# Reading counts and lists out of PSUM at once, gathered rows in a ring of tiles, and gathers issued earlier, in a recurrence-and-router kernel

## The chip, the cores and the metric

The kernel runs on one core of a Trainium2 chip. The metric is the device time of one execution in microseconds (us). The core has a matrix engine (TensorE, PE in the profile, with its weight loads on a row of their own, PEld), a vector engine (VectorE, DVE), a scalar engine (ScalarE, ACT), a general engine (GpSimd, POOL) and a queue engine that issues transfers (SyncE, SP). The engines run side by side, each through its own list of instructions in order, and wait for one another where data or buffers demand it. Matrix products land in PSUM, a small memory that DVE and ACT read out; all else lies in SBUF.

## The reference, cut to what matters

Inputs are float32. There are two stages. The first is a linear recurrence over 768 steps for 4 batches and 8 heads of width 48; the second is a router that sends each of the 3072 rows of width 384 to the one of 8 experts with the largest logit, and runs that expert's two layers.

```python
for t in range(S):                                   # S = 768
    kt, vt, rt = (k[:, :, t], v[:, :, t], r[:, :, t])
    cur = np.einsum('bhd,bhe->bhde', u[None] * kt, vt)
    y[:, :, t] = np.einsum('bhd,bhde->bhe', rt, state + cur)
    state = w[None, :, :, None] * state + np.einsum('bhd,bhe->bhde', kt, vt)
x = y.transpose(0, 2, 1, 3).reshape(B * S, H * D)    # 3072 x 384

logits = xn @ en.T / tau                             # xn, en: rows of x and of the embeddings, normalised
expert_idx = np.argmax(logits, axis=1)
gate_w = softmax(logits)[np.arange(N), expert_idx]
for e in range(E):                                   # E = 8
    mask = expert_idx == e
    h = np.maximum(x[mask] @ w1[e], 0.0)             # 384 -> 1024
    out[mask] = gate_w[mask, None] * (h @ w2[e])     # 1024 -> 384
```

## The kernel before

The recurrence is done in 24 units: unit i is chunk i // 4 (128 steps) of batch i % 4. A loop over i works on several units at once at different stages (a software pipeline). After every fourth unit the chunk's 512 rows are routed: `choose` finds the expert, `ranks` the place in that expert's list, `slices` and `taken` put row numbers and gates into the lists (`k.sums`). The rows themselves go to a buffer `xs` in the chip's main memory (`put`), from where each expert gathers its own.

After chunk 3 (unit 15 and those before it), the counts are read once (`counted`, at j = 7) and the two experts with the fewest rows so far (ranks 7 and 6, `LAST`) are settled as the first to run (`settle`). Their weights are loaded during the last units, and the first 128 rows of each ("early" rows) are gathered from `xs` and run through the expert at the loop's end. Then the final lists are made, and the experts run one after the other: the two of `LAST` with their remaining rows, then the six others.

Each tile of PSUM in the first stage comes from `Banks`: a tag has one buffer (two for "tp" and "at"). A new tile with a tag waits until the last reader of the tile before it, with the same tag, is done. The tag "st" is used by `states`, `ranks`, `taken`, `counted` and the first `turned_lists`.

```python
def counted(k):
    cp = k.ps.tile([128, E], F32, name="cp", tag="st")
    k.nc.tensor.matmul(cp, k.ones, k.cum, start=True, stop=True)
    return cp

def order(k, cp, settled=None):
    load = p.tile([128, E], F32, name="load", tag="load")
    nc.vector.tensor_sub(load, cp, k.tie)                     # L582: reads cp
    ...                                                       # key, more, by (L586 to L593)
    return load, by

def settle(k, cp):
    load, by = order(k, cp)
    ...                                                       # settled (L603), expert_of: eq, is_e, who
    nc.vector.tensor_sub(lack, cp[0:1, :], k.ebase)           # L607: reads cp
    ...

def ranks(k, g):
    g.rank = k.ps.tile([128, B, E], F32, name="rank", tag="st")
    mm(g.rank, k.umask, g.oh, start=True, stop=False)         # L496
    ...

def taken(k, g):
    g.take = k.ps.tile([QS, 128], F32, name="take", tag="st")
    ...                                                       # 4 matmuls, L563

def taken_by_rank(k, lists):
    take = tiles(k, lists, E * TM)                            # L833, L835: read lists
    gates = k.const.tile([128, E * TM], F32, name="gates", tag="gates", bufs=2)
    k.nc.vector.tensor_copy(gates, lists[:, 1, :])            # L651: reads lists
    return take, gates

def attention(k):
    for i in range(-1, units + 7):
        ...                                                   # summed, places, own_rows, turn, ...
        whole(choose, i - 3)
        whole(listed, i - 5)
        on(sums, i)
        on(carry, i)
        on(rows, i)
        of_group(put, i)
        on(scores, i + 1)
        on(own_sum, i + 1)
        of_group(turn_rows, i - 1)
        of_group(logits, i - 2)
        whole(ranks, i - 3)
        whole(gates, i - 3)
        whole(taken, i - 5)
        ...
        j = i - SETTLED * B                                   # SETTLED * B = 12
        if j == 7:
            k.cp = counted(k)
        if j == 8:
            settle(k, k.cp)
            for w, r in zip(k.weights, LAST):
                load_weights_of(k, r, w)
        if j == 9:
            perm = turner(k, k.by)
            k.lists = turned_lists(k, perm, "st")             # L644
        if j == 10:
            lists = taken_by_rank(k, k.lists)
            first = [Early(k, r, *lists, w) for r, w in zip(LAST, k.weights)]
            to = outs(k, lists[0], E * TM)
        if i == units - 1:
            for f in first:
                f.turn()
        ...                                                   # first[0]: hidden, rows, out; first[1].hidden(0)
    cp = counted(k)
    loads, by = order(k, cp, k.settled)
    lists = turned_lists(k, turner(k, by), "lg")
    first[1].hidden(1)
    k.take, k.gates = taken_by_rank(k, lists)
    k.to = outs(k, k.take, E * TM)
    first[1].rows(0)
    first[1].rows(1)                                          # L815
    first[1].out(to)                                          # L822 and L823: earlyy to the output
    caps_passed(k, loads, by)
```

`Early` zeroes a tile of its own (L782) and gathers into it (L783). After the first stage its pools are closed, and the pools of the expert stage (`gp`, `xtp`, `hp`) take the same part of SBUF. A gather zeroes its tile on DVE, because rows past the end of a list are not written:

```python
def gather(k, take, to, gate, n=128):
    G = k.gp.tile([128, DM], F32, name="G", tag="G")          # 8 buffers
    nc.vector.memset(G, 0.0)                                  # L856
    nc.gpsimd.indirect_dma_start(out=G[0:n, :], in_=k.xs[:, :], ...)   # L857
    return G, to, gate, n

def expert(k, rows, w1, w2):
    ...
    for m in range(NK):
        for t, (G, _, _, here) in enumerate(rows):
            nc.tensor.transpose(ps[...], G[0:here, ...], k.ident[...])  # L873
        nc.vector.tensor_copy(xT[:, m, 0:n], ps[:, 0:n])               # L876
    ...                                                       # first layer L881, L882; second L899 or L889 to L896
```

Of the kernel before, what the change touches and what calls it, by code (L numbers as in the profile page):

```python
# [19 lines left out]
C = 128  # L20
NCH = S // C
DP = 64
NP = H // 2
# [22 lines left out]
def build_first(k):  # L46


    nc, pool = k.nc, k.aconst
    wc = pool.tile([128, NP], F32, name="wc")  # L50
    nc.vector.memset(wc, 1.0)
    with nc.allow_non_contiguous_dma(reason="384 words"):
        for s, q in ((0, nc.sync), (1, nc.scalar)):
            q.dma_start(out=wc[s * DP : s * DP + D, :], in_=k.w.rearrange("(p s) d -> s d p", s=2)[s])
    k.ones = k.const.tile([128, 128], F32, name="ones")
    nc.vector.memset(k.ones, 1.0)
    wide = pool.tile([128, 512], F32, name="wide")
    nc.vector.memset(wide, 1.0)
    k.ident = k.const.tile([128, 128], F32, name="ident")
    make_identity(nc, k.ident)  # L60

    def wake(count):
        ps = k.ps.tile([128, 512], F32, name="wake", tag="y")
        for _ in range(count):
            nc.tensor.matmul(ps, k.ones, wide, start=True, stop=True)

    wake(WAKE[0])
    for lst, name, count in ((k.Kpad, "Kpad", 4), (k.Rpad, "Rpad", AHEAD + 2)):
        for i in range(count):
            t = pool.tile([128, H, DP], F32, name=f"{name}{i}")  # L70
            nc.gpsimd.memset(t[:, :, D:DP], 0.0)
            lst.append(t)
    load(k, 0, nc.scalar)


    nc.vector.tensor_scalar(wc, wc, W_MIN, W_MAX, ALU.max, ALU.min)
    t = pool.tile([128, NP, C], F32, name="wpow")
    for p in range(NP):
        nc.vector.tensor_tensor_scan(
            t[:, p, :], wc[:, p : p + 1].to_broadcast([128, C]), k.ones, 1.0, ALU.mult, ALU.mult  # L80
        )
    mid = pool.tile([128, NP], F32, name="mid")
    nc.vector.reciprocal(mid, t[:, :, C // 2])
    over_i = mid[:, :, None].to_broadcast([128, NP, C])
    kp = pool.tile([128, NP, C], F32, name="kp")
    nc.vector.tensor_mul(kp, t[:, :, ::-1], over_i)
    ps = k.ps.tile([128, NP, 2, DP], F32, name="kpT", tag="xp")
    for p in range(NP):
        nc.tensor.transpose(ps[:, p].rearrange("q s d -> q (s d)"), kp[:, p, :], k.ident)
    wake(WAKE[1])  # L90
    k.rpow = pool.tile([128, NP, C], F32, name="rpow")
    nc.vector.tensor_mul(k.rpow, t, over_i)
    cols = ps[:, :, :, 0:D]
    nc.vector.tensor_mul(
        k.Kpad[0].rearrange("q (p s) d -> q p s d", s=2)[:, :, :, 0:D],
        k.loaded[0][0].rearrange("q (p s) d -> q p s d", s=2), cols,
    )
    k.kpow = pool.tile([128, H, D], F32, name="kpow")
    nc.vector.tensor_copy(k.kpow.rearrange("q (p s) d -> q p s d", s=2), cols)  # L99
    k.wC = t[:, :, C - 1 : C].to_broadcast([128, NP, D])  # L100
# [10 lines left out]
def build_consts(k):  # L111
# [35 lines left out]
    k.turned = numbers(k, "turned", [QS, QS], [[0, 2], [1, E], [0, TM]], 1, 0)  # L147
    k.part = pool.tile([QS, 1], I32, name="part")
    nc.gpsimd.iota(k.part, pattern=[[0, 1]], base=0, channel_multiplier=1)
    k.caps = pool.tile([1, E], F32, name="caps")  # L150
    for i, cap in enumerate(CAPS):
        nc.gpsimd.memset(k.caps[:, i : i + 1], float(cap))
# [50 lines left out]
def build_experts(k):  # L203

    nc, pool = k.nc, k.aconst
    emb, tau = k.emb_rows, k.tau_rows
    sq = pool.tile([E, DM], F32, name="emb_sq")
    nrm = pool.tile([E, 1], F32, name="emb_nrm")
    nc.scalar.activation(sq, emb, ACT.Square, accum_out=nrm)
    nc.gpsimd.tensor_tensor(out=nrm, in0=nrm, in1=k.half[0:E, 0:1], op=ALU.pow)  # L210
    yield
    nc.vector.tensor_scalar_add(nrm, nrm, 1e-6)
    nc.vector.reciprocal(nrm, nrm)
    nc.vector.reciprocal(tau, tau)
    nc.vector.tensor_scalar(emb, emb, nrm, tau, ALU.mult, ALU.mult)
    yield
    ps = k.ps.tile([128, NK, E], F32, name="ps", tag="xp")
    for c in range(NK):
        nc.tensor.transpose(ps[:, c, :], emb[:, c * 128 : (c + 1) * 128], k.ident[0:E, 0:E])
    k.ent = k.const.tile([128, NK, E], F32, name="ent")  # L220
    nc.vector.tensor_copy(k.ent, ps)
    yield
# [352 lines left out]
    return cp  # L575


def order(k, cp, settled=None):

    nc, p = k.nc, k.rt  # L580
    load = p.tile([128, E], F32, name="load", tag="load")
    nc.vector.tensor_sub(load, cp, k.tie)  # L582
    key = load
    if settled is not None:
        key = p.tile([128, E], F32, name="key", tag="key")
        nc.vector.scalar_tensor_tensor(key, settled, -float(4 * N), load, ALU.mult, ALU.add)  # L586
    more = p.tile([128, E, E], F32, name="more", tag="more")
    full = [128, E, E]
    nc.vector.tensor_tensor(
        more, key[:, None, :].to_broadcast(full), key[:, :, None].to_broadcast(full), ALU.is_gt  # L590
    )
    by = p.tile([128, E], F32, name="by", tag="by")
    nc.vector.reduce_sum(by, more, axis=AX.X)  # L593
    return load, by


def settle(k, cp):


    nc, pool = k.nc, k.const  # L600
    load, by = order(k, cp)
    k.settled = pool.tile([128, E], F32, name="settled")
    nc.vector.tensor_scalar(k.settled, by, float(min(LAST)) - 1, None, ALU.max)  # L603
    expert_of(k, by)
    k.by = by
    lack = pool.tile([1, E], F32, name="lack")
    nc.vector.tensor_sub(lack, cp[0:1, :], k.ebase)  # L607
    nc.vector.tensor_scalar(lack, lack, -1.0, 128.0, ALU.mult, ALU.add)
    last = pool.tile([1, E], F32, name="last")
    nc.vector.tensor_scalar(last, by[0:1], float(min(LAST)), None, ALU.is_ge)  # L610
    nc.vector.scalar_tensor_tensor(lack, lack, 0.0, last, ALU.max, ALU.mult)
    nc.vector.tensor_add(k.cum[0:1], k.cum[0:1], lack)
# [74 lines left out]
def attention(k):  # L687
# [4 lines left out]
    def on(f, i):  # L692
        if 0 <= i < units:
            f(k, i)
# [8 lines left out]

    emb = build_experts(k)
    for i in range(-1, units + 7):
        if 0 < i + AHEAD < units:
            load(k, i + AHEAD)
        if i < 2:
# [8 lines left out]
        of_group(squares, i - 1)  # L717
        whole(choose, i - 3)
        whole(listed, i - 5)
        on(sums, i)  # L720
        on(carry, i)
        on(rows, i)
# [9 lines left out]
            decays(k)  # L732
        if i == 2:
            build_turned(k)
        j = i - SETTLED * B
        if j == 7:
            k.cp = counted(k)
        if j == 8:
            settle(k, k.cp)
            for w, r in zip(k.weights, LAST):  # L740
                load_weights_of(k, r, w)
        if j == 9:
            perm = turner(k, k.by)
            k.lists = turned_lists(k, perm, "st")
        if j == 10:
            lists = taken_by_rank(k, k.lists)
            first = [Early(k, r, *lists, w) for r, w in zip(LAST, k.weights)]
            to = outs(k, lists[0], E * TM)
        if i == units - 1:
            for f in first:  # L750
# [7 lines left out]
        if i == units + 4:  # L758
            first[0].rows(1)
            first[0].out(to)  # L760
            first[1].hidden(0)
    cp = counted(k)
    loads, by = order(k, cp, k.settled)
    lists = turned_lists(k, turner(k, by), "lg")
    first[1].hidden(1)
    k.take, k.gates = taken_by_rank(k, lists)
    k.to = outs(k, k.take, E * TM)
    first[1].rows(0)
    first[1].rows(1)
    first[1].out(to)  # L770
    caps_passed(k, loads, by)


class Early:


    def __init__(self, k, r, take, gates, weights):
        self.k, self.r, self.weights = k, r, weights
        self.col = slice(r * TM, r * TM + 1)
        self.gate = gates[:, self.col]  # L780
        self.G = k.aconst.tile([128, DM], F32, name=f"early{r}")
        k.nc.vector.memset(self.G, 0.0)  # L782
        k.nc.gpsimd.indirect_dma_start(  # L783
            out=self.G[:, :], out_offset=None, in_=k.xs[0 : (SETTLED + 1) * B * C, :],
            in_offset=IndirectOffsetOnAxis(ap=take[:, self.col], axis=0),
# [4 lines left out]
    def turn(self):  # L790
        k, nc = self.k, self.k.nc
        ps = k.ps.tile([128, NK, 128], F32, name="early_x", tag="tp")
        for m in range(NK):
            nc.tensor.transpose(ps[:, m, :], self.G[:, m * 128 : (m + 1) * 128], k.ident)
        self.xT = k.aconst.tile([128, NK, 128], F32, name=f"earlyx{self.r}")
        nc.vector.tensor_copy(self.xT, ps)

    def hidden(self, half):
# [19 lines left out]

    def out(self, to):
        k, nc, ps = self.k, self.k.nc, self.ps  # L820
        y = k.aconst.tile([128, DM], F32, name=f"earlyy{self.r}")
        nc.vector.tensor_scalar_mul(y, ps, self.gate)  # L822
        nc.gpsimd.indirect_dma_start(  # L823
            out=k.out[:, :], out_offset=IndirectOffsetOnAxis(ap=to[:, self.col], axis=0), in_=y[:, :], in_offset=None,
# [27 lines left out]
def gather(k, take, to, gate, n=128):  # L852

    nc = k.nc
    G = k.gp.tile([128, DM], F32, name="G", tag="G")
    nc.vector.memset(G, 0.0)  # L856
    nc.gpsimd.indirect_dma_start(  # L857
        out=G[0:n, :], out_offset=None, in_=k.xs[:, :], in_offset=IndirectOffsetOnAxis(ap=take[0:n], axis=0),
        bounds_check=N - 1, oob_is_err=False,
    )  # L860
    return G, to, gate, n


def expert(k, rows, w1, w2):
# [146 lines left out]
def kernel(  # L1011
# [47 lines left out]
    with ExitStack() as ctx2:  # L1059
        expert_pools(n, ctx2)  # L1060
        for i, r in enumerate(TURN):
            at = [
                gather(n, *(a[:, j : j + 1] for a in (n.take, n.to, n.gates)), min(128, CAPS[r] - t))
                for t, j in zip(range(0, CAPS[r], 128), range(r * TM, (r + 1) * TM))
                if t > 0 or r not in LAST
            ]
            expert(n, at, *n.weights.pop(0))
            if i + 2 < E:
                n.weights.append(weight_tiles(n))
                load_weights_of(n, TURN[i + 2], n.weights[-1])  # L1070
# [29 lines left out]
```

## Time and profile before

| | |
|---|---|
| Device time, median of 3 runs | 514.47 us (507.24, 516.09, 514.47) |
| The profiled execution | 508.23 us, of which the span from first to last instruction is 506.1 us |
| PE busy | 468.6 us (93% of the span) |
| DVE, ACT, POOL busy | 162.2, 123.0, 167.4 us |
| First stage and early rows | to 226.15 us, the end of the early rows' last matmul |
| Expert stage | from 234.5 us, its first transposes, to the end |

How to read it: "busy" is the time in which an engine has an instruction in it, and for PE the ends of matmuls are modelled. The span in 40 slices has one digit for each slice of 12.65 us, the busy share in tenths; PEclk is the clock that TensorE was granted, in tenths of full speed. A line of the waits names the engine and line that waited, what it waited for, and the time in all, the number of times, and the longest. The chain of work that ended last runs back from the last instruction, at each step to what released it. A table by windows gives for each stretch its length, then the busy time and number of instructions of PE, PEld, DVE, ACT and POOL, then the granted clock as a share, the share of DMA time, and GB/s.

### The profile page before, as it was taken

The page shows a single profiled execution, that of the slowest core. Times are in us where ns is not written, and L with a number is a line of the kernel's source. Part 1 is how long each engine was busy: PE and PEld are TensorE (multiplying, and loading weights), DVE is VectorE, ACT ScalarE, POOL GpSimd, SP SyncE. Part 2 cuts the span into 40 slices and gives each one's busy share as a digit, 9 for nine tenths or more (in the row PEclk, how much of TensorE's full clock was granted, in tenths as well). Part 3 has the DMA queues.
Part 4 walks back from the last instruction along what each step waited for, and adds up shares of the span by engine and source line. Part 5 has one row for each costly group of instructions (what it writes and reads, how often), then busy time and mean ns, then how long its engine had stood idle before and what let it go on. Part 6 is the DMA issues. An engine that isn't in the chain of part 4 may idle for free.

```text
span 506.1 us, 7084 instructions
## 1 busy us (share of the span) xinstructions
PE 468.6 (93%) x2620; PEld 346.7 (68%) x2620; DVE 162.2 (32%) x442; ACT 123.0 (24%) x382; POOL 167.4 (33%) x250
## 2 busy tenths in 40 slices
PE   8899999999997979974999999999999999999991
PEld 3899999999996878753767555555555555555550
DVE  5676666666567442324020300400400300102000
ACT  2455544553454321100201020120120120110200
POOL 6766574857657021205230400150140211001010
PEclk9999999999999775996999999999999999999996
DMA  8865554454420950003354603433423423400000
GB/s 182 175 131 126 126 117 98 101 126 102 103 64 32 347 215 16 1 16 103 103 207 164 200 8 118 142 97 124 142 95 124 151 64 128 141 16 30 0 35 19
DMA packets 93790, 54.25 MB, mean 107 GB/s; under 512 B 76937, under 2 KB 88380, under 8 KB 93746
## 3 DMA queue, kind: packets, MB, share of 16 engines
q1 hardware_dynamic: 89024, 43.85, 31.2%
q0 software_dynamic: 3296, 9.44, 5.5%
q10 hardware_dynamic: 1426, 0.41, 0.3%
q8 instruction: 23, 0.38, 0.3%
q14 instruction: 21, 0.17, 0.1%
HBM read 44.45 MB, written 9.63 MB: 107 GB/s over the span
## 4 chain that ended last, share of the span: by engine, by line
PE 49%; DVE 2%; DMA 1%; issue 0%; POOL 0%; POOLq 0%; DVEq 0%
PE ps L881 24%; PE ps L899 13%; PE ps L889 10%; DVE y L901 1%; PE ps L896 1%; DMA G<-xs,take 1%; PE ps L873 1%; DVE xTe L876 1%; DMA out_dram<-earlyy,to 1%; DVE G L856 0%; POOL out_dram L902 0%; POOLq L942 0%; DVEq L856 0%
## 5 line engine op out<-in xcount | busy, mean ns | idle before, releaser
L881 PE MATMUL ps<-xTe,w 128*128 128x384 f32 (+3 forms) x384 | 123.3, 482 | 2.8 <-DVE xTe L876 2.8
L881 PEld LDWEIGHTS ps<-xTe,w 128*128 128x128 f32 x384 | 74.0, 194 | 48.9 <-issue 21.7
L902 POOL DMA_INDIRECT out_dram<-y,to x25 | 24.8, 994 | 205.8 <-DVE y L901 186.9
L901 DVE TENSOR_SCALAR y<-ps,gates 128x384 f32<-128x384 f32 (+2 forms) x25 | 14.6, 613 | 226.7 <-PE ps L899 127.4
L882 ACT ACTIVATE hT<-ps 128x384 f32<-128x384 f32 (+3 forms) x64 | 30.6, 478 | 176.3 <-PE ps L881 158.1
L899 PE MATMUL ps<-w,hT 128*128 128x384 f32 x208 | 67.9, 486 | 0.0
L899 PEld LDWEIGHTS ps<-w,hT 128*128 128x128 f32 x208 | 39.5, 190 | 27.1
L889 PE MATMUL ps<-hT,w 128*128 128x416 f32 (+1 forms) x144 | 52.0, 521 | 0.0
L289 ACT ACTIVATE xd<-V,diag 128x48 f32<-128x48 f32 x192 | 45.9, 321 | 20.1 <-DVE diag L281 14.5
L367 PE MATMUL y<-V,AT 128*128 128x48 f32 x384 | 47.5, 278 | 0.0
L367 PEld LDWEIGHTS y<-V,AT 128*128 128x128 f32 x384 | 46.6, 198 | 0.0
L889 PEld LDWEIGHTS ps<-hT,w 128*128 128x128 f32 x144 | 27.4, 190 | 24.2 <-issue 24.2
L321 DVE TENSOR_TENSOR AT<-at,umask 128x512 f32<-128x512 f32 x48 | 30.9, 686 | 13.5 <-PE at L317 13.5
L351 POOL TENSOR_TENSOR state<-state,wpow 48x192 f32<-48x192 f32 x40 | 20.4, 510 | 31.9 <-DVE state L347 30.4
L317 PE MATMUL at<-RT,KT 48*128 48x128 f32 x384 | 27.9, 285 | 2.0 <-ACT KT L306 2.0
L857 POOL DMA_INDIRECT G<-xs,take x25 | 25.4, 1016 | 12.7 <-issue 5.2
L460 ACT COPY xT<-xp 128x384 f32<-128x384 f32 x24 | 11.5, 480 | 67.1 <-PE xp L458 67.1
L317 PEld LDWEIGHTS at<-RT,KT 48*128 48x128 f32 x384 | 23.3, 187 | 3.7 <-ACT KT L306 2.6
L275 POOL TENSOR_TENSOR KU<-KU,Rpad 128x384 f32<-128x384 f32 x24 | 24.1, 1003 | 1.9
L266 POOL TENSOR_TENSOR Kpad<-K,kpow 128x384 f32<-128x384 f32 x23 | 23.0, 999 | 3.8 <-DVE kpow L99 2.5
L274 POOL TENSOR_TENSOR KU<-K,u_bc 128x384 f32<-128x384 f32 x24 | 24.0, 1001 | 0.4 <-DVE load L582 0.4
L380 DVE TENSOR_TENSOR X<-y,xd 128x384 f32<-128x384 f32 x24 | 13.4, 558 | 30.8 <-PE y L367 27.3
(179 smaller groups left out, 513.2 us busy)
## 6 DMA issues: line engine op xcount, KB each, us to landing
w<-in_moe_w_dram SPq DMA_DIRECT2D x16, 1536.0 KB, 6.9
K<-in_k_dram SPq DMA_DIRECT2D x24, 192.0 KB, 3.5
V<-in_v_dram SPq DMA_DIRECT2D x24, 192.0 KB, 3.6
xs<-X SPq DMA_DIRECT2D x24, 192.0 KB, 2.0
Rpad<-in_r_dram SPq DMA_DIRECT2D x23, 192.0 KB, 3.7
G<-xs,take POOLq DMA_INDIRECT x25, 3.1
out_dram<-y,to POOLq DMA_INDIRECT x25, 2.6
Rpad<-in_r_dram ACTq DMA_DIRECT2D x1, 192.0 KB, 3.9
```

Of the source, the lines that this page charges most:

```text
L274: nc.gpsimd.tensor_mul(KU, K, k.u_bc)
L275: nc.gpsimd.tensor_mul(KU, KU, R[:, :, 0:D])
L289: k.nc.scalar.mul(xd[:, h, :], V[:, h, :], diag[:, h : h + 1])
L317: nc.tensor.matmul(at[s][:, p, :], KT[rows, p, :], RT[rows, p, :], start=True, stop=True)
L321: nc.vector.tensor_mul(a, at[s], k.umask[:, None, :].to_broadcast([128, NP, C]))
L367: mm(y[:, h, :], AT[h % 2][:, h // 2, :], V[:, h, :], start=first, stop=(h == H - 1), skip_group_check=True,)
L857: nc.gpsimd.indirect_dma_start(out=G[0:n, :], out_offset=None, in_=k.xs[:, :], in_offset=IndirectOffsetOnAxis(ap=take[0:n], axis=0), bound ...
L881: mm(ps[:, 0:n], w1[:, m, f * 128 : (f + 1) * 128], xT[:, m, 0:n], start=(m == 0), stop=(m == NK - 1))
L882: nc.scalar.activation(hT[:, f, 0:n], ps[:, 0:n], ACT.Relu)
L889: mm(ps[:, 0:n], w2[:, f, m * 128 : (m + 1) * 128], hT[:, f, 0:n], start=(f == 0), stop=(f == NF - 1))
L899: mm(ps, hT[:, f, at], w2[:, f, :], start=(f == 0), stop=(f == NF - 1))
L902: nc.gpsimd.indirect_dma_start(out=k.out[:, :], out_offset=IndirectOffsetOnAxis(ap=to[0:here], axis=0), in_=y[0:here, :], in_offset=None, ...
```

## The change

It has three parts, and a fourth that makes room for them.

1. The counts and the first lists are read out of PSUM right after the matmul that makes them. `loads` reads the counts into two SBUF tiles at j = 7; before, they were read at j = 8, some of them late in `settle`. The lists made at j = 9 are read at j = 10 ahead of that iteration's `sums`, not at its end. The buffer of tag "st" is then free sooner.
2. Gathered rows live in a ring of eight tiles that is allocated with the constants. Each is zeroed once, on GpSimd, in iterations 3 to 10; a gather zeroes nothing any more. What lies in a tile past a list's end is then the rows of an earlier gather, and those results are not written out. The early rows use the ring too, so `Early` has no zeroing of its own.
3. The gathers of the first two experts are issued inside the first stage, as soon as the final lists are read and ahead of the early rows' last matmuls.
4. Several tiles of the first stage (`wide`, `kp`, the squares of the embeddings, the early rows' turned and output tiles) move into buffers of the work pool, which pays for the ring.

```diff
-def order(k, cp, settled=None):
+def loads(k):
     nc, p = k.nc, k.rt
+    cp = counted(k)
     load = p.tile([128, E], F32, name="load", tag="load")
     nc.vector.tensor_sub(load, cp, k.tie)
+    count = p.tile([1, E], F32, name="counts", tag="counts")
+    nc.vector.tensor_sub(count, cp[0:1, :], k.ebase)
+    return load, count
+
+def order(k, load, settled=None):
 ...
-    nc.vector.tensor_sub(lack, cp[0:1, :], k.ebase)
-    nc.vector.tensor_scalar(lack, lack, -1.0, 128.0, ALU.mult, ALU.add)
+    nc.vector.tensor_scalar(lack, count, -1.0, 128.0, ALU.mult, ALU.add)
 ...
+    k.ring, k.turns = [pool.tile([128, DM], F32, name=f"G{i}") for i in range(8)], 0
 ...
         whole(choose, i - 3)
         whole(listed, i - 5)
+        if j == 10:
+            lists = taken_by_rank(k, k.lists)
+            first = [Early(k, r, *lists, w) for r, w in zip(LAST, k.weights)]
         on(sums, i)
 ...
+        if 3 <= i < 3 + len(k.ring):
+            k.nc.gpsimd.memset(k.ring[i - 3], 0.0)
         if j == 7:
-            k.cp = counted(k)
+            load_, count = loads(k)
         if j == 8:
-            settle(k, k.cp)
+            settle(k, load_, count)
 ...
         if j == 10:
-            lists = taken_by_rank(k, k.lists)
-            first = [Early(k, r, *lists, w) for r, w in zip(LAST, k.weights)]
             to = outs(k, lists[0], E * TM)
 ...
     k.take, k.gates = taken_by_rank(k, lists)
+    k.rows_of = {r: gathers(k, r) for r in LAST}
     k.to = outs(k, k.take, E * TM)
     first[1].rows(0)
     first[1].rows(1)
 ...
-        self.G = k.aconst.tile([128, DM], F32, name=f"early{r}")
-        k.nc.vector.memset(self.G, 0.0)
+        self.G = k.ring[k.turns % len(k.ring)]
+        k.turns += 1
 ...
-        y = k.aconst.tile([128, DM], F32, name=f"earlyy{self.r}")
+        y = k.work.tile([128, DM], F32, name="earlyy", tag="xd")
 ...
 def gather(k, take, to, gate, n=128):
-    G = k.gp.tile([128, DM], F32, name="G", tag="G")
-    nc.vector.memset(G, 0.0)
+    G = k.ring[k.turns % len(k.ring)]
+    k.turns += 1
 ...
         for i, r in enumerate(TURN):
-            at = [gather(...) ...]
-            expert(n, at, *n.weights.pop(0))
+            rows = n.rows_of.pop(r) if r in LAST else gathers(n, r)
+            expert(n, [...], *n.weights.pop(0))
```

## The prediction

> **What bounds the kernel now.** I read the page's first two parts, then the waits of PE, then the chain that ended last, then a table of 2 us windows around the waits, then the timeline there.
>
> The page says that PE is the engine to follow:
>
> ```profile
> PE 468.6 (93%) x2620; PEld 346.7 (68%) x2620; DVE 162.2 (32%) x442; ACT 123.0 (24%) x382; POOL 167.4 (33%) x250
> PE   8899999999997979974999999999999999999991
> PEclk9999999999999775996999999999999999999996
> ```
>
> The reader is to see, counting slices of 12.65 us from 0, that PE dips in slices 12, 14, 17 and 18 and its clock in 13 to 15 and 18, so in 152 to 240 us and on the heels of PE's idle time. Everywhere else both are full. So what frees PE there moves the end; nothing else does.
>
> PE's own waits:
>
> ```profile
> PE ps L873 <- DMA G<-xs,take: 8.9, 2, 8.4
> PE take L563 <- DVE lack L607: 3.7, 1, 3.7
> ...
> PE rank L496 <- DVE gates L651: 2.7, 1, 2.7
> PE lists L644 <- DVE perm L638: 2.6, 2, 1.5
> ```
>
> Three of the four are what the change is aimed at. L563 and L496 need nothing that L607 and L651 compute: they wait for the one "st" buffer, whose last readers these are. The wait for `perm` is for data, and the change leaves it.
>
> The chain, where the stages meet:
>
> ```profile
> 227.09 2.59 DMA out_dram<-earlyy,to
> ...
> 232.20 0.39 DVE G L856
> 232.59 0.09 issue
> 232.68 3.01 DMA G<-xs,take
> 235.69 0.04 issue
> 235.73 1.11 PE ps L873 x4
> 236.85 12.92 PE ps L881 x48
> ...
> 261.13 10.63 PE ps L881 x48
> ```
>
> The early rows' output has to leave SBUF before the gather tiles, which take its place, can be zeroed; then come zeroing, gather, transposes. The same 48 matmuls take 12.92 us for the first expert and 10.63 for the second.
>
> The windows tell why, and what the short waits cost beside their own length:
>
> ```profile
> 162.00:164.00 2.00, 0.47 (x3) 0.50 (x4) 1.83 (x9) 0.53 (x3) 1.70 (x2) 0.79 0.00 0
> 164.00:166.00 2.00, 2.00 (x10) 1.67 (x9) 0.31 (x2) 0.00 (x0) 0.00 (x0) 0.50 0.45 51
> ...
> 186.00:188.00 2.00, 2.00 (x11) 2.00 (x11) 0.10 (x1) 0.00 (x0) 1.45 (x5) 0.50 0.65 176
> ...
> 200.00:202.00 2.00, 2.00 (x17) 2.00 (x16) 0.00 (x0) 0.00 (x0) 0.00 (x0) 0.83 0.00 0
> ```
>
> The third number from the right (0.79 in the first line) is the granted clock. It falls to 0.50 after each wait: at about 163 us for 3 us, at 174 for 3, at 184 for 17, at 232 for 9.5. At 0.50 half as many instructions pass (x11 in 2 us).
>
> **What the Trainium skill says.** *TensorE: Matmul & The Clock Gate*, section "What's actually happening": the clock is passed at half rate by default and at full rate after a busy window of about 3.4 us, and falls back after an idle one; the window runs free. The trace agrees on the two levels (0.50 and 1.00) but not fully on the trigger: here waits of 3.7, 2.7 and 1.1 us each precede a fall, one of 1.5 us at 216 us does not, and the 17 us at half rate held while PE was nearly always busy. *DMA: Bandwidth & Descriptors*, "Anatomy of one DMA — SWDGE (gpsimd) path": about 2.0 us plus bytes over 436 GB/s; a gather of 196,608 bytes would be 2.5 us as an estimate from that page, the trace has 3.1 as median. *SBUF — State Buffer*, "Who interferes with whom": GpSimd and DVE share one pair of ports, and a GpSimd instruction that only writes leaves a two-input DVE instruction alone. So the ring's zeroing should slow DVE little; no run before shows it in that place.
>
> **The change part by part.**
>
> *Counts.* At 159.80 us PE had finished its unit and wanted "st" for L563; it got it at 163.53, after L607. The two reads (0.16 and 0.14 us) now follow the count's matmul (it ends at 154.12), while DVE stands between two other instructions; they delay DVE's next by 0.3 us, beside a later wait of 1.3 us for ACT. L563's inputs were ready at 157.25. So 3.7 us go. After that PE runs ahead of DVE, which is busy with `settle` until about 163.6; the next unit's RT is then made at about 164.6 and PE wants it at about 165.3, so I see no new wait, with 0.7 us to spare. The half clock from 163 to 166.3 goes too: L563's group took 1.97 instead of 1.09 (as at 209.56), the rt transposes 1.11 instead of 0.64, kt 0.73 instead of 0.60: 1.4, of which I count 1.3.
>
> *Lists.* PE waited 2.69 us for "st" at L496 until 183.47. The lists were ready at 173.4, and DVE, whose work before that point ended at 176.2, waited 2.6 us before L380. Three reads (0.19, 0.19, 0.18) fit into that wait. 2.7 us go. The two early gathers start some 8 us sooner, beside the weight load (400 GB/s until 182 us); they have 8 us before PE needs them.
>
> *The long half clock, 184 to 201.* At full rate it would not save half of 17 us, since PE would meet other waits. The three rank matmul groups take 2.17 us there and 1.2 at 205.60. From their end (185.64) to L563's group at 196.47 are 10.8 us. Walked at full rate: y 1.03 + 1.91, xp and lg 1.28, early_x 1.0; then DVE copies the early rows, makes tile, place, lane and sel (about 2.0 us), GpSimd the two products 0.8: 8.0 us, so 2.8 saved. L563's group saves 0.9, the 12 matmuls of L804 1.1 (4.04 to 2.92). With the rank groups 1.0: 5.8 in all, if the clock stays up. I count 5.5.
>
> *Gathers.* The final lists were read by 218.57 us and the early rows' matmuls ended at 226.15. GpSimd needs 1.3 us for each gather (1.02 and 0.3 between), two tiles for the first expert, 3.1 to land: both in by 224.5, so hidden. The transposes follow the early rows at once. For the second expert the same transposes and first layer ran from 259.93 to 271.76, 11.83 us at full rate. One thing is worse: in the instructions' new order, DVE does earlyy (0.62), eq and is_e (0.2 each) ahead of the first copy L876, and two more small ones between the copies: about 1.3 us. So 13.1 us from 226.15, where it was 23.6 (to 249.77): 10.5 go, with the half clock of 232 to 241 in them. The early rows' output now stands behind eight gathers on GpSimd and leaves some 2 us later; nobody waits for it.
>
> *Zeroing.* Eight GpSimd memsets at 0.41 us (as those of `state`, L135) in iterations of about 6 us in which GpSimd is busy for 4 to 6; a little may come through in the two iterations with gates. The 25 DVE memsets at 0.38 us save nothing beside PE in the expert stage.
>
> Sum: 3.7 + 1.3 + 2.7 + 5.5 + 10.5 = 23.7, less 1.0 for small new waits: 22.7. Span 506.1 - 22.7 = 483.4, and 2.1 for what lies outside the span (508.23 - 506.1): 485.5.
>
> **The rivals.** *The clock falls all the same.* The wait of 1.1 us for `perm` at 172 stays, and before the fall at 174 stood only that. If the clock falls there and stays down until the dense matmuls of L804, the 5.5 are not saved and some 3 more are lost on the unit after: 491 to 494. For it speaks that the timed runs before scatter by 9 us; a half clock from 163 through to 201 would make about 7 us more than the profiled run (38 us at half cost 19 instead of the 11.7 that (3.3 + 2.7 + 17.3) / 2 gives), about 515, which is where two of the three runs lie. *A new wait takes the old one's place.* DVE's `settle` chain has 0.7 us to spare before PE wants RT; if it is later, up to 2 us of the 3.7 come back: 487.5. *The handover is bound by something else in reused SBUF*, the first xTe or hT waiting for a transfer out of the early rows: in the new order these wait for loads and stores long done, not for that transfer, so I give it little; it would cost 3 to 5 us: 489. *GpSimd's zeroing delays the units*: 3.3 us in all, at worst 487.
>
> **Range and chances.** 485.5 if all holds, 491 to 494 with the clock down; I weigh these about three to one and get 487. If the fall at 174 goes as well (1.7 us) it is below 484. Range 481.5 to 496. Within 2% of 514.47 means above 504: all of the first stage's gain would have to fail and part of the handover's.
>
> **What would show it.** Right: no wait of PE L563 on L607 or L496 on L651; PEclk 1.00 over 160 to 172; the first transposes within 0.5 us of the early rows' last matmul; first layer of the first expert near 10.7 us; from there to the end 256 us as before (506.1 - 249.77). Wrong: PE waiting for RT or for the early gathers; a first L876 released by a DMA; the clock at 0.50 for over 10 us between 165 and 195; units longer than 6 us where the ring is zeroed.

## The result and the profile after

The changed kernel takes 486.88 us (median of 486.77, 486.74, 486.99 and 494.63) where the kernel before takes 511.50 (median of 507.24, 516.09, 514.47 and 508.53). The ratio is put at 0.9544, the middle of its 95% interval of 0.9428 to 0.966. The profiled execution has a span of 485.0 us, against 506.1: 21.1 us less.

The page's first two parts, for the changed kernel:

```profile
PE 462.1 (95%) x2620; PEld 341.6 (70%) x2620; DVE 151.7 (31%) x416; ACT 122.5 (25%) x382; POOL 170.7 (35%) x258
PE   8899999999999999899999999999999999999990
PEclk9999999999999976989999999999999999999996
```

PE has the same 2620 instructions. The dips of PE to 7 and to 4 are gone, but PEclk still shows a 7, a 6 and an 8 in slices 14, 15 and 17 (of 12.1 us each): the clock still falls, though PE is now nearly always busy.

PE's waits in the changed kernel (time in all, times, longest):

```profile
PE lists L653 <- DVE perm L647: 2.6, 2, 1.5
...
PE take L564 <- POOL what L553: 0.8, 1, 0.8
PE ps L895 <- issue: 0.7, 1, 0.7
```

The waits for the "st" buffer (3.7 and 2.7 us) and for the gathers (8.9) are gone. What is left of the handover is 0.7 us at L895, the first transposes; the wait for `perm` is as before.

The chain that ended last, where the stages meet:

```profile
211.22 5.16 PE early_y L828 x16
218.10 10.63 PE ps L903 x48
228.73 10.33 PE ps L921 x32
```

Between the early rows and the first expert's first layer stand no transfer and no zeroing any more, only transposes and copies. The first layer takes 10.63 us, as the second expert's did before.

The windows around the last units:

```profile
172.00:174.00 2.00, 2.00 (x28) 1.88 (x24) 1.54 (x3) 0.48 (x1) 1.67 (x3) 1.00 1.07 411
174.00:176.00 2.00, 2.00 (x20) 2.00 (x19) 1.38 (x7) 0.56 (x3) 1.47 (x5) 1.00 1.03 425
176.00:178.00 2.00, 2.00 (x14) 2.00 (x13) 1.07 (x8) 1.98 (x9) 0.10 (x1) 0.62 1.02 417
178.00:180.00 2.00, 2.00 (x11) 2.00 (x12) 0.56 (x1) 0.62 (x2) 0.00 (x0) 0.50 1.04 389
```

Here is the one surprise. The granted clock (0.62, then 0.50) falls at 176.5 us and stays down to 190.1, and PE has been busy 2.00 us of every 2 before it. No wait brought it down. What PE ran in the last 3.4 us before the fall (start, busy, what; `x6` is six instructions, two for each float32 matmul, and 128x8 is what streams through, 8 columns of 128):

```profile
173.11 0.73 PE L474 MATMUL lg<-ent,xT 128*128 128x8 f32 x6
173.70 0.39 PE L497 MATMUL rank<-oh,umask 128*128 128x32 f32 x2
173.92 0.81 PE L499 MATMUL rank<-oh,ones 128*128 128x24 f32 x6
174.59 0.39 PE L500 MATMUL rank<-cum,ones 128*128 128x32 f32 x2
174.81 1.11 PE L365 MATMUL y<-state,RT 128*128 128x96 f32 x8
175.76 2.87 PE L368 MATMUL y<-V,AT 128*128 128x48 f32 x16
```

All of it is narrow: 8 to 96 columns.

### The profile page after: what moved, and what is told of

It reads as the page before. It is cut to its first block, busy times and chain, and to the rows that moved or that the text cites. A ratio compares the mean times of both kernels' runs of the same rounds, so it can differ in the third digit from the quotient of the medians.

```text
span 485.0 us, 7056 instructions
## 1 busy us (share of the span) xinstructions
PE 462.1 (95%) x2620; PEld 341.6 (70%) x2620; DVE 151.7 (31%) x416; ACT 122.5 (25%) x382; POOL 170.7 (35%) x258
## 3 DMA queue, kind: packets, MB, share of 16 engines
q1 hardware_dynamic: 89024, 43.85, 32.5%
## 4 chain that ended last, share of the span: by engine, by line
PE 85%; DVE 6%; ACT 2%; DMA 2%; SPq 2%; issue 1%; POOL 1%; ACTq 0%; POOLq 0%; DVEq 0%
PE ps L903 25%; PE ps L921 14%; PE ps L911 11%; PE y L368 8%; PE at L318 5%; PE y L365 4%; PE st L335 3%; PE early_h L817 3%; PE lg L474 2%; DVE AT L322 2%; PE rt L300 2%; PE xp L459 2%; PE early_y L828 2%; PE take L564 1%; DVE y L923 1%; PE kt L305 1%
## 5 line engine op out<-in xcount | busy, mean ns | idle before, releaser
L903 PE MATMUL ps<-xTe,w 128*128 128x384 f32 (+3 forms) x384 | 120.9, 475 | 3.0 <-DVE xTe L898 2.8
L903 PEld LDWEIGHTS ps<-xTe,w 128*128 128x128 f32 x384 | 72.3, 190 | 48.3 <-issue 22.3
L335 PE MATMUL st<-V,Kpad 128*128 128x96 f32 x160 | 21.0, 274 | 0.9 <-DVE at L519 0.9
```

The costliest lines, as they stand in the source:

```text
L335: nc.tensor.matmul(st[:, p, :], pair(Kw, p), pair(V, p), start=True, stop=True)
L903: mm(ps[:, 0:n], w1[:, m, f * 128 : (f + 1) * 128], xT[:, m, 0:n], start=(m == 0), stop=(m == NK - 1))
```

## The experiments

The profiled executions of two kernels (k3 and k8) have, besides, a half clock of 13.7 us in the first units that the others do not have; where a span below holds it, that is said. Each ratio is to the kernel before, measured beside that test (medians of 508.5 to 508.8 us), and is the middle of its 95% interval.

**Counts alone (k1).** On the kernel before:

```diff
-        if j == 7:
-            k.cp = counted(k)
+            load_, count = loads(k)          # reads cp at once
         if j == 8:
-            settle(k, k.cp)
+            settle(k, load_, count)
```

> The kernel before with the counts alone read at once. If the wait on the one buffer and the half clock behind it are all this read costs, PE's wait of L563 on DVE (3.7 us) and the half clock at 163 us (1.3 us) go, and the span is 506.1 - 5.3 = 500.8 us. Theory A (a wait of PE brings the clock down): the long half clock at the last unit stays, since the wait of the rank matmuls (2.7 us) stays. Theory B (it is the last units' own matmuls, with few columns each, that bring it down): it stays too. Rival: DVE's chain in settle is now waited for, and less than 3 us is gained.

Measured: span 499.4, ratio 0.9896 (0.9869 to 0.9923). It cannot tell theory A from theory B, which expect the same of it. The wait of L563 is gone, and so is the half clock at 163. The one at 174 went too, which I had not counted; that is the 1.4 us more than foretold. The wait of the rank matmuls (2.69 us) is there, and a half clock from 177.1 to 194.2. No wait for DVE took the old one's place.

**Counts and lists (k2).** The same, and the first lists read ahead of `sums`:

```diff
         whole(listed, i - 5)
+        if j == 10:
+            lists = taken_by_rank(k, k.lists)
+            first = [Early(k, r, *lists, w) for r, w in zip(LAST, k.weights)]
         on(sums, i)
 ...
         if j == 10:
-            lists = taken_by_rank(k, k.lists)
-            first = [Early(k, r, *lists, w) for r, w in zip(LAST, k.weights)]
             to = outs(k, lists[0], E * TM)
```

> The kernel before with counts and lists both read at once, gathers as before. Theory A (waits bring the clock down): both waits gone, the clock stays at 1.00 through the last units, early rows end near 226.15 - 14 = 212 us, span near 491. Theory B (the last units' matmuls bring it down by themselves): a half clock of over 10 us after about 176 us though PE has not waited before it; early rows end near 216.4 us, span near 506.1 - 9.8 = 496.3.

Measured: span 493.3, ratio 0.9874 (0.9813 to 0.9935). Its executions lie between 495.43 and 504.28 us, those of k1 between 501.41 and 504.11, so the times alone do not separate the two; the traces do. Its windows:

```profile
174.00:176.00 2.00, 2.00 (x20) 2.00 (x20) 1.25 (x4) 0.34 (x1) 1.93 (x3) 1.00 1.05 428
176.00:178.00 2.00, 2.00 (x18) 2.00 (x18) 1.52 (x11) 1.55 (x8) 0.60 (x3) 0.87 1.04 426
178.00:180.00 2.00, 2.00 (x12) 2.00 (x12) 0.72 (x2) 1.56 (x7) 0.00 (x0) 0.50 1.02 387
```

Both "st" waits are gone and the clock falls nevertheless, at 177.5, with PE full, for 10 us. Theory A, which is the prediction's, falls here. The early rows end at 213.64, better than theory B's 216.4, because the changed kernel's second fall (at 207) does not come in this execution, though PE's wait of 1.45 us for `perm` stands there as well.

**Ring and early gathers alone (k3).** The changed kernel with counts and lists read late, as before.

> The changed kernel with counts and lists read late again, as before; ring and early gathers stay. If the parts add up, the first stage is as before (early rows' end near 226 us, waits of 3.7 and 2.7 us) and the handover as after: 506.1 - 11.3 = 494.8 us span. Rival: part of the handover's gain needs the shorter first stage (gathers not landed in time), then 497 or more.

Measured: 498.40 us (median of five), ratio 0.9791 (0.9771 to 0.981). The profiled execution (503.4) holds the half clock of the first units, so only its handover is compared: from the early rows' end (234.78) to the end of the first layer (247.13) are 12.35 us, in the changed kernel 12.34 (216.39 to 228.73), before 23.62. The handover's gain does not depend on the first part. Expected were 496.9 (494.8, and 2.1 outside the span); the three fastest of its five executions take 495.69, 497.15 and 498.40, the other two 505.3. So the parts add up, as far as this scatter lets one see.

**Ring without the early issue (k4).** The changed kernel, with the gathers of the first two experts after the early rows' output:

```diff
-    k.rows_of = {r: gathers(k, r) for r in LAST}
     k.to = outs(k, k.take, E * TM)
 ...
     first[1].out(to)
+    k.rows_of = {r: gathers(k, r) for r in LAST}
```

> The changed kernel with the ring, but the first two experts' gathers issued after the early rows' output. If being early is what counts: the first transposes wait for earlyy, one issue of 1.3 us and 3.1 us landing per tile, so they start some 5 to 6 us after the early rows' end (0.7 in the changed kernel), the clock falls once more for about 2 us of loss; span 485.0 + 7 = 492. If the ring (no wait for reused memory, no zeroing) is what counts: within 2 us of 485.0.

Measured: span 498.6, ratio to the kernel before 0.9863 (0.9844 to 0.9882). The timeline of PE at the handover, first of this kernel, then of the changed one (start, busy, what, and in brackets the idle time before it and what ended it):

```profile
227.67 0.66 PE L895 MATMUL ps<-ident,G 128*128 128x128 f32 x2 [5.51 <-DMA G<-xs,take]
229.07 1.11 PE L895 MATMUL ps<-ident,G 128*128 128x128 f32 x4 [0.74 <-DMA G<-xs,take]
```

```profile
217.09 0.88 PE L895 MATMUL ps<-ident,G 128*128 128x128 f32 x6 [0.71 <-issue]
```

The handover takes 20.10 us (222.17 to 242.27) against 12.34: lateness costs 7.8 of the 11.3 us, and the ring by itself is worth the other 3.5. About 2.3 of the 7.8 are the clock, at half from 226.4 to 233.2 behind the wait of 5.51 us: the transposes take 1.77 us for 0.88, the first layer 12.09 for 10.63. The other 5.8 us of the 13.6 were lost ahead of the early rows' end (222.17 for 216.39), where both kernels have the same instructions: in this execution the clock fell at 168 us already, and stayed down to 196. Its four executions lie between 500.49 and 502.63 us, so the early fall seems to be the rule for this kernel; what makes it so is not known.

```profile
166.00:168.00 2.00, 1.01 (x8) 0.94 (x9) 0.90 (x5) 1.33 (x6) 0.00 (x0) 1.00 1.03 422
168.00:170.00 2.00, 2.00 (x15) 2.00 (x12) 1.78 (x9) 1.64 (x6) 0.00 (x0) 0.60 1.03 399
```

The first line has PE busy for only 1.01 us of 2: unlike the fall at 176.5, this one comes behind a wait, the 1.11 us for `perm`.

**What brings the clock down: dense and sparse fill (k5, k6).** The changed kernel, with matmuls whose result is not used at three places: at i = units - 2 ahead of the rank matmuls and behind them, and at i = units - 1 after the logits. In k5 one of 512 columns each, in k6 five of 8.

```diff
+def fill(k):
+    ps = k.ps.tile([128, 512], F32, name="fill", tag="tp")
+    for _ in range(1):                                        # k6: range(5)
+        k.nc.tensor.matmul(
+            ps[:, 0:512], k.ones, k.rpow.rearrange("p a b -> p (a b)")[:, 0:512], start=True, stop=True
+        )                                                     # k6: 0:8 in both places
 ...
+        if i in (units - 2, units - 1):
+            fill(k)
         whole(ranks, i - 3)
+        if i == units - 2:
+            fill(k)
```

> The changed kernel plus three filling matmuls of 512 columns (1.2 us each as the first ones of the kernel, 3.5 in all; their result is not used), two around the rank matmuls of the unit before the last and one after the last unit's logits. Theory B (few columns bring the clock down, and keep it down): no half clock in the last units, or one shorter than 7 us; the fill's 3.5 us are paid and about 5.4 us of half clock saved; span 481 to 485. Theory A (PE's waits) and theory C (the weight load at 400 GB/s beside it): half clock of 10 us or more from about 177 us as in the changed kernel, span 488 to 491.

> The same three places filled with five matmuls of 8 columns each (about as long as one of 512, as the logits' matmuls show: 0.24 us each). PE is as busy as with the dense fill. Theory B: the half clock comes as in the changed kernel and stays for 10 us or more; span 488 to 492. If being busy without a wait is what counts: as the dense fill, 481 to 485.

Measured: the dense fill has a span of 481.4, 3.6 us faster than the changed kernel, though it does more; its ratio to the kernel before is 0.9486 (0.9377 to 0.9595). The sparse fill has 488.9. The same windows, dense first, then sparse:

```profile
172.00:176.00 4.00, 4.00 (x38) 3.40 (x38) 2.90 (x8) 0.79 (x3) 2.68 (x3) 1.00 1.05 415
176.00:180.00 4.00, 4.00 (x33) 3.52 (x32) 1.51 (x10) 2.23 (x10) 0.84 (x4) 1.00 1.03 408
```

```profile
172.00:176.00 4.00, 4.00 (x44) 3.83 (x43) 2.85 (x7) 0.60 (x2) 2.87 (x3) 1.00 1.06 415
176.00:180.00 4.00, 4.00 (x27) 4.00 (x26) 1.31 (x9) 2.41 (x11) 0.86 (x4) 0.68 1.03 407
```

PE is full in all four lines. With wide matmuls the clock stays at 1.00, with narrow ones it falls at 177.4 and comes back at 194.5. That is theory B: what counts is not that PE holds an instruction, but how much it streams. The last column but one shows the weight load going on in both. Nor is it the place of the clock's steps, which come at multiples of 3.41 us (see below): counted back from the falls at the end of the work (474.0 and 481.2 us), they lie within 0.4 us of each other in the two executions. In three of four executions of the dense fill the mean clock is 0.992 or 0.993, in one it is 0.965; where the clock fell in that one is not known. All four of the sparse fill are at 0.975 or below, and so are the four of the changed kernel (0.974 or below). The spans of those three executions are 481.1 to 481.4 us, of the changed kernel's three near ones 485.0 to 485.2, but the two were measured at different times, and the intervals of their ratios overlap.

**The weight load (k7).** The changed kernel, with the two settled experts' weights loaded at j = 0 under fixed numbers, so the rows of these two ranks go through the wrong weights.

```diff
+        if j == 0:
+            for w, e in zip(k.weights, (0, 1)):
+                load_weights(k, e, w)
         if j == 8:
             settle(k, load_, count)
-            for w, r in zip(k.weights, LAST):
-                load_weights_of(k, r, w)
```

> The changed kernel with the first two experts' weights loaded at j = 0 under fixed numbers (experts 0 and 1), so that no weight load runs beside the last units; the rows of these two ranks go through the wrong expert's weights. Theory C (the load brings the clock down): clock at 1.00 over the last units, early rows end near 216.4 - 6 = 210 us, span near 479 to 481. Theory B: half clock for over 10 us all the same, span 484 to 487 (the loop may shift by a few tenths).

```profile
168.00:172.00 4.00, 4.00 (x25) 4.00 (x22) 2.03 (x10) 1.75 (x7) 1.29 (x1) 0.58 0.00 0
172.00:176.00 4.00, 4.00 (x26) 3.69 (x26) 1.13 (x2) 0.00 (x0) 2.04 (x2) 0.50 0.48 148
176.00:180.00 4.00, 4.00 (x21) 4.00 (x20) 3.02 (x15) 2.76 (x11) 0.36 (x2) 0.50 0.00 0
```

The last number is GB/s. No weights are on the way, only the early rows' two gathers and a unit's store, and the clock is down from 168.6 to 195.9, with PE full until 188. So the load is not needed to keep the clock down. Whether it helps to bring it down where PE has not waited stays open: this fall has the wait of 1.11 us for `perm` in the 3.41 us before it, and those without a wait (176.5 us in the changed kernel, 177.5 in k2, 177.4 in k6) all have the load beside them. The span is 490.9 us; those of other executions of this kernel are 478.9 to 485.3, with mean clocks up to 0.992, so the fall does not come every time, and the best of them is where theory C has it (479 to 481).

**Two instructions moved (k8).** For the second fall, at 207 us:

```diff
-    lists = turned_lists(k, turner(k, by), "lg")
     first[1].hidden(1)
+    lists = turned_lists(k, turner(k, by), "lg")
 ...
     first[1].rows(1)
+    caps_passed(k, load_, by)
     first[1].out(to)
-    caps_passed(k, load_, by)
```

> The changed kernel with two instructions moved: the second half of the second early expert's first layer stands ahead of the final lists' matmul, so that PE has work while DVE makes perm; and the check on list lengths (caps_passed) ahead of the early rows' output, so that DVE is free for the first xTe. PE's wait for perm of 1.5 us goes, and if the fall of the clock at 207 us comes from that place, its 1.65 us too; the handover loses about 0.5 us of DVE. The gathers start 1.4 us later and are still landed in time. Span 485.0 - 3.6 = 481.4; without the fall's part 483.

```profile
211.15 2.92 PE L817 MATMUL early_h<-earlyx,w 128*128 128x128 f32 x24
214.00 0.43 PE L653 MATMUL lists<-perm,sums 64*128 64x64 f32 x2
```

Measured: 486.91 us, ratio 0.9505 (0.9396 to 0.9614); the profiled execution, 488.4, holds the half clock of the first units. The three fastest of its six executions have spans of 480.9, 482.1 and 482.1, where 481.4 was expected. No bracket stands behind the lists' matmul: the wait of 1.5 us is gone, and the clock stays up behind it. That the wait brought the fall at 207 is not shown by this alone: in k2 and k5 the same wait is there and the clock stays up too. From the counts' matmul to the early rows' end are 8.79 us (211.01 to 219.80), 11.85 in the changed kernel: 3.06 saved. Moving `caps_passed` brought nothing, since the handover is 12.34 as before: the first transposes wait for the early rows' output to be read out of its bank (0.71 us), which stands ahead of it.

**All of it (k9).** k8's moves; the first lists' matmul behind the next unit's transposes; dense fills, the third now ahead of the last `take`:

```diff
         on(turn, i + 1)
+        if j == 10:
+            k.lists = turned_lists(k, perm, "st")
 ...
+        if i == units:
+            fill(k)
         whole(taken, i - 5)
 ...
         if j == 9:
             perm = turner(k, k.by)
-            k.lists = turned_lists(k, perm, "st")
```

> The changed kernel with everything that helped: the two instructions moved as in the last test, the first lists' matmul moved behind the next unit's transposes (its wait of 1.1 us for perm goes), and three fills of 512 columns, two around the rank matmuls and one ahead of the last chunk's take, where PE waits for GpSimd anyway. From the changed kernel's 485.0: 3.1 us for the moved instructions, 1.1 for the lists, 3.6 for the dense fill as measured and about 1 more for the third fill's better place: span 476.2. Theory B: no half clock between 160 and 220 us. If the third fill's place leaves the clock to fall in the last unit: 480 to 483.

Measured: 479.45 us, ratio to the kernel before 0.9426 (0.9396 to 0.9455), span 477.2 where 476.2 was expected. There is no half clock in the first 468 us:

```profile
PEclk9999999999999999999999999999999999999996
```

Of the two waits for `perm` one of 0.2 us is left. Five of its six executions take 478.95 to 479.70 us, one 487.30; of the changed kernel's four, measured at another time, three take 486.74 to 486.99. So this version is faster than both kernels, by about 7 us against the changed one.

**Fill in the first units too (k10).** As k9, with `i in (0, 1, units - 2)` for the first fill.

> The same with a fill of 512 columns after each of the first two units' logits, where two profiled executions (the changed kernel's gathers alone, and the moved instructions) show a half clock of 13 us from 21 us on that the others do not have. Theory B: that half clock comes no more, so the scatter between executions falls from some 10 us to under 4; if PE has gaps there anyway (it is busy 3.3 of 4 us), the fastest execution loses under 1.5 us: span 476 to 478. If the early half clock has another cause, the scatter stays at 6 us or more.

Measured: 482.09 us, ratio 0.9487 (0.9453 to 0.952), span 478.5. Its six executions lie within 4.2 us (480.27 to 484.43), those of k9 within 8.4 (478.95 to 487.30). The fastest loses 1.3 us and the median 2.6: not worth it. The scatter is smaller, as theory B has it, but six executions are few, the 4 us I named were just missed, as was the span of 476 to 478, and k9's profile has no early half clock either, so that the fills take it away is not shown.

## Why the prediction was right, and where it was not

The time (487.0 foretold, 486.88 measured) is nearer than the working deserves, and that is luck: 487 is a weighting of two cases, 485.5 and 491 to 494, and neither came as it was described. Term by term, from where the same matmul stands in the two profiles:

| Step | Foretold, us | Measured, us | From |
|---|---|---|---|
| Counts: the wait | 3.7 | 4.0 | L563 at 163.53, now 159.57 |
| the half clock behind it | 1.3 | 1.3 | the first lists at 172.93, now 167.63: 5.3 in all |
| Lists: the wait | 2.7 | 2.7 | no wait before the rank matmuls |
| the half clock at 174 | 0 | 1.8 | rank at 183.47, now 173.70: 9.8 in all, so 4.5 with the wait |
| The long half clock | 5.5 | 1.6 | the counts at 215.94, now 204.54: 11.4 in all |
| a new half clock at 207 | 0 | -1.6 | early rows' end 226.15, now 216.39: 9.8 in all |
| Gathers | 10.5 | 11.3 | first layer's end 249.77, now 228.73: 21.0 in all |
| Allowance | -1.0 | 0.1 | span 506.1, now 485.0 |
| Sum (the terms measured are rounded) | 22.7 | 21.1 | |

**Counts and lists** held as foretold, with RT ready in time (it was made at 163.49 to 164.16, and the matmul that reads it began at 164.31). k1 shows the counts alone, k2 both together.

**The long half clock** is the step that failed. The prediction put it behind the wait of 2.7 us and had it stay away with the wait gone. The wait went and the fall came all the same, shorter by 3.4 us (13.7 for 17.1), so that the term of 5.5 us measured 1.6; the prediction had named "the clock at 0.50 for over 10 us between 165 and 195" as a sign of being wrong. k2 shows it on the kernel before, k5 against k6 that the last units' narrow matmuls (8 columns in the logits, 8 to 32 in rank, 96 and 48 in y) bring it without a wait, and k7 that it stays down without the weight load. Neither the load nor the number of instructions tells the falling stretch from the one before it in the changed kernel: from 169.67 to 173.08 us PE is full with 38 instructions and 395 GB/s beside it, from 173.08 to 176.49 it is full with 33 and 421 GB/s, and only the second, which has next to nothing of 128 columns in it, is followed by a fall. That PE could be faster there was right: from the rank matmuls to the counts' are 32.5 us before, 30.8 in the changed kernel and 27.5 with the dense fill, two fills (1.1 us each) included. The prediction's rival "the clock falls all the same" came nearest, but not by its path, a fall at 174 behind the wait for `perm` that stays (the clock was at 1.00 there), and not with its 491 to 494: the fall at 174, left out of the sum, went after all (1.8), and the handover gave 0.8 more than foretold.

**The gathers** held. k4 divides their 11.3 us: 7.8 from issuing them ahead, 3.5 from the ring. What the prediction put down to the order of DVE's small instructions, 1.3 us, is 0.5 (12.34 for the 11.83 of the second expert), and it is not their order: the transposes begin 0.71 us after the early rows' last matmul, where `earlyy` has been read out, and not within the 0.5 foretold; eq and is_e run while they do. The early rows' output left 0.8 us after its tile was ready, behind the eight gathers, and nobody waited for it.

**Zeroing** on GpSimd took 0.42 us each (foretold 0.41), and the first 150 us are the same in both kernels (the counts' matmul at 153.75 and 153.59). Of *SBUF — State Buffer*, "Who interferes with whom", no run here is a test: the DVE instruction that the memset at 43.07 us overlaps (L381, 0.56 us in both kernels) reads one of its two inputs from PSUM.

On the clock, *TensorE: Matmul & The Clock Gate*, "What's actually happening", has busy and idle windows of about 3.4 us. In the profile before, the clock changes at 163.15, 166.56, 173.39, 176.80, 183.63 and 200.69: each step is a multiple of 3.41 us, so the windows agree (and the half clocks that the prediction read as about 3 and 9.5 us are 3.41 and 10.24). That "busy" means what the profile calls busy does not: in the changed kernel the window before 176.5 has no idle PE in it.

Still open is which amount of streaming keeps the clock up, and how short waits add to it: the falls at 168 in k4 and k7 have a wait of 1.11 us in the window before them, the one at 207 a wait of 1.46, and elsewhere the same waits bring none. That the fall's place depends on where the windows lie over the narrow matmuls and waits fits k4 (168) beside the changed kernel (176.5) with the same instructions, but it was argued and not set by a test.

## What to carry to other kernels

A tile with one PSUM buffer and late readers can make the matrix engine wait at some later matmul that has nothing to do with it: read the result into SBUF right behind the matmul, and look for such waits by their releaser, not by the data. Work at a change of stages (gathers above all) can be issued while the old stage still runs if its tiles do not lie in memory that the old stage holds. And on the matrix engine judge stretches of narrow matmuls by the granted clock, not by busy time: a wide matmul more can be cheaper than none.

## What the hardware showed that I had not expected

The clock falls to 0.50 with TensorE busy throughout, behind a stretch of matmuls with 8 to 96 columns (at 176.5 us), and in the changed kernel comes back at 190.1 us, 4 us into matmuls of 128 columns. Within an execution it changes at multiples of 3.41 us. Three matmuls of 512 columns, 3.3 us of work, made the kernel 3.6 us faster in the profiled execution; fifteen of 8 columns made it 3.9 us slower.
